# A new hand-order table for an RWKV-5 block fused with a squared-ReLU MLP: same steps, other engine orders, PSUM banks, fillers and squares

## The chip, the cores and the metric

One core of a Trainium2 chip runs the whole program. The metric is the device time of one execution in microseconds: of the kernel before, the median of three runs. Five engines work side by side, each through its own list of instructions in order: TensorE (PE; its weight loads are PEld), VectorE (DVE), ScalarE (ACT), GpSimd (POOL) and SyncE (SP). SP does nothing here but start transfers; POOL and ACT start some too. All transfers of the core share 16 DMA engines. Matrix products land in PSUM, eight banks of 128 partitions by 512 floats; the other operands lie in SBUF.

## The reference

First an attention-like recurrence over 768 steps for 4 batches and 8 heads of 48 columns, then a two-layer MLP on its 3072 rows:

```python
for t in range(S):
    cur = np.einsum('bhd,bhe->bhde', u[None] * kt, vt)
    y[:, :, t] = np.einsum('bhd,bhde->bhe', rt, state + cur)
    state = w[None, :, :, None] * state + np.einsum('bhd,bhe->bhde', kt, vt)
...
h = x @ w_in            # 3072 x 384 by 384 x 2048
g = np.maximum(h, 0.0) ** 2
return g @ w_out        # 2048 x 384
```

Inputs and output are float32.

## The kernel before

**Tiling.** The 768 steps are cut into 6 chunks of 128; a chunk of one batch is a *unit*, and there are 24 of them, numbered chunk by chunk (units 0 to 3 are the four batches of chunk 0). Within a unit the recurrence is done in matrix form: r and k are scaled by powers of w (`scale`, L301/L303), turned so that the head's columns lie on partitions (`turn` and `rkT` through PE and ACT for units 0 to 5; one transposing transfer `rkD`, L322, for a pair of units from 6 on), multiplied into a 128 by 128 table per head (`at`, L369), masked to its triangle (`mask`, L377), multiplied with v (`y`, L441) and with the state of the chunks before (L447). `rk` and `d` (L357/L360, L389/L410) give the diagonal that u weights, `dv` (L420) and `yb` (L456) add it, and `s`, `sadd`, `sdec`, `stb` (L398, L424, L428, L432) carry the state on. `xturn`/`xT` or the transposing transfer `xD` (L467) turn y into the MLP's input. `m1` (L493) is the first product, `relu` (L501, ACT) takes it out of PSUM as f32, the square goes to ACT (`sqA`, L508) or DVE (`sqD`, L510), `m2` (L517) is the second product in four quarters per unit, `osb` (L524, ACT) takes its 128 by 384 result out, and `out` (L553, SP) stores it. Unit 23, the last, has its second product in two pieces (`m2.23.0`, `m2.23.1`, L533) with an eviction each (`osb.23.0` on ACT, L543; `osb.23.1` on DVE, L545) and a store each (`out.23.0`, `out.23.1`, L549).

**What sets the order.** Nothing is scheduled by the compiler: the string `ORDER` lists every step as a word, and the loop at the end of the kernel runs through it and issues the step's instructions. Each engine executes its own instructions in the order in which their words stand; words of different engines only wait for each other through the data. `name.unit.part@banks` gives the PSUM bank of a matmul step. `fill.N` issues N matmuls on a constant tile whose result nobody reads (L216). An instruction that isn't ready holds all that stands behind it on its engine. That goes for SP too: a store waits there for its eviction, and every later transfer of SP waits behind it.

**Buffers.** Evicted output rows (`osb`) rotate through 6 SBUF buffers, evicted hidden tiles (`gr`) through 6, loaded pairs of r, k and v through 4. An eviction `osb` that gets a buffer for the second time waits until the store of the former content has landed. The `osb` of the two pieces of unit 23 have one buffer each of their own.

```python
mpool = ctx.enter_context(tc.tile_pool(name="mpool", bufs=6))
...
tiles[i]["osb"] = mpool.tile([128, dm], F32, name="osb")
nc.scalar.copy(tiles[i]["osb"], tiles[i]["o"])
...
nc.sync.dma_start(out=out[b * S + c * C : b * S + (c + 1) * C, :], in_=tiles[i]["osb"])
```

Of the kernel before, what the change touches and what calls it, by code (L numbers as in the profile page):

```python
# [26 lines left out]
relu.0.1 s.3@7 xT.2 d.3@6 sqD.0.1 at.3@40 relu.1.1 turn.4.1@2 mask.3.1 m1.2.2@1 vb.4 rkT.4.1 dv.3 m1.2.3@5 relu.2.2
mask.3.0 at.4@02 vb.5 rk.4 m2.0.0@6 relu.2.3 mask.4.0 sqA.2.2 m1.2.1@1 sqD.2.3 relu.1.3 m1.2.0@4 mask.4.1 sqA.0.2
sqD.1.3 m2.1.0@5 stb.2 relu.2.0 sadd.3 kb.4@0 y.3@3 relu.2.1 sqD.1.1 y.4@2 stb.3 m2.0.1 yb.3 kbT.4 scale.5.0 m2.1.1
sqA.2.0 sqD.2.1 kt.8 xturn.3@4 s.4@7 xT.3 turn.5.0@1 sadd.4 m2.1.2 rkT.5.0 dv.4 m1.3.1@3 sdec.4 kt.10 yb.4 m1.3.0@0  # L30
stb.4 relu.3.1 scale.6.0 m2.0.2 scale.5.1 relu.3.0 xturn.4@4 scale.7.0 m2.0.3 sqA.3.0 rt.8 sqD.3.1 xT.4 m1.3.3@1
osb.0 scale.6.1 turn.5.1@7 out.0 relu.3.3 m1.4.0@2 scale.7.1 rkT.5.1 m2.3.0@3 sqD.3.3 relu.4.0 rkD.6 m1.4.3@0 rk.5
sqA.4.0 kb.5@4 relu.4.3 at.5@61 m1.4.2@7 kbT.5 mask.5.0 vtS.6 m1.4.1@2 sqD.4.3 relu.4.2 mask.5.1 m2.3.1 sqA.4.2
s.5@0 relu.4.1 y.5@4 dv.5 m2.1.3 sqA.4.1 vtS.8 sadd.5 m1.3.2@6 yb.5 osb.1 sdec.5 out.1 relu.3.2 m2.2.0@7 scale.8.0
stb.5 scale.8.1 m2.2.1 rt.10 sqA.3.2 scale.9.0 m2.2.2 scale.9.1 m2.2.3 m2.3.2 osb.2 rkD.8 rk.6 at.6@1205 xturn.5@4
mask.7.1 m2.4.0@6 xT.5 out.2 mask.6.1 m2.4.1 vb.6 mask.7.0 rt.12 m1.5.3@7 mask.6.0 s.6@5 relu.5.3 s.7@4 dv.6 y.7@2
y.6@0 dv.7 m2.4.2 sqD.5.3 vtS.10 vb.8 m1.5.0@1 yb.6 yb.7 m2.4.3 relu.5.0 sadd.7 xD.6 m1.5.1@7 scale.10.0 sqA.5.0
scale.10.1 m2.3.3 osb.4 relu.5.1 sdec.7 out.4 m1.5.2@0 scale.11.1 osb.3 stb.7 m2.5.0@2 scale.11.0 sqA.5.1 sadd.6
out.3 at.8@1467 relu.5.2 rk.8 rkD.10 m2.5.1 sqA.5.2 mask.8.0 s.8@3 mask.8.1 s.9@5 kt.12 m2.5.2 sdec.6 y.8@0 sadd.8
stb.6 m2.5.3 scale.12.0 mask.9.0 osb.5 sadd.9 out.5 mask.9.1 kt.14 vb.10 m1.6.0@1 sdec.9 dv.8 m1.6.4@4 relu.6.0  # L40
scale.13.0 m1.6.3@2 yb.8 vtS.12 sqA.6.0 sdec.8 m1.6.6@6 relu.6.4 dv.9 relu.6.3 m1.6.7@7 sqA.6.4 sqD.6.3 m1.6.1@3
relu.6.7 rk.10 rt.14 y.9@1 relu.6.6 m1.6.2@0 sqD.6.7 stb.9 relu.6.1 yb.9 at.10@4527 relu.6.2 scale.12.1 s.11@6 xD.8
m1.6.5@3 sqA.6.1 mask.11.1 sqA.6.2 s.10@1 dv.11 m2.6.0@0 vtS.14 relu.6.5 dv.10 m2.6.1 scale.13.1 sqA.6.6 mask.10.0
sqA.6.5 m2.7.0@7 stb.8 rkD.12 mask.11.0 m2.7.1 mask.10.1 m2.7.2 sadd.10 vb.12 m2.6.2 sadd.11 kt.16 sdec.10 m2.6.3
sdec.11 y.10@3 osb.6 y.11@4 stb.10 yb.10 out.6 m2.7.3 stb.11 yb.11 m1.8.0@2 scale.14.0 osb.7 xD.10 scale.14.1
m1.8.1@5 relu.8.0 scale.15.0 m1.8.7@1 scale.15.1 sqA.8.0 out.7 m1.8.3@6 relu.8.1 kt.18 relu.8.7 m1.8.2@0 sqA.8.1
kt.20 sqD.8.7 m1.8.6@3 relu.8.2 m2.8.0@4 relu.8.3 sqA.8.2 m1.8.4@7 sqD.8.3 relu.8.6 at.12@2510 rk.12 relu.8.4 m2.8.1
mask.13.1 sqA.8.6 rkD.14 s.12@6 mask.12.0 sqA.8.4 m1.8.5@3 vb.14 mask.12.1 s.13@7 m1.10.5@0 relu.8.5 sadd.12 rt.16
sadd.13 y.12@2 sqA.8.5 sdec.12 m1.10.6@5 relu.10.5 sdec.13 m2.8.2 stb.12 mask.13.0 sqA.10.5 m1.10.3@3 vtS.16 dv.13
relu.10.6 m1.10.0@0 dv.12 relu.10.3 yb.12 m1.10.1@1 sqA.10.6 sqD.10.3 relu.10.0 y.13@7 vtS.18 m1.10.7@5 relu.10.1  # L50
yb.13 sqA.10.0 m2.8.3 xD.12 relu.10.7 m1.10.4@6 osb.8 sqD.10.7 stb.13 m1.10.2@3 out.8 rk.14 relu.10.4 at.14@2017
vtS.20 relu.10.2 m2.9.0@5 sqA.10.4 mask.14.0 sqA.10.2 s.15@4 mask.15.1 m2.9.1 sqA.10.1 dv.15 rt.18 m2.9.2 sadd.15
m2.11.0@6 mask.15.0 vb.16 sdec.15 m2.11.1 scale.16.0 m2.11.2 scale.16.1 rt.20 m2.11.3 scale.17.0 mask.14.1 s.14@3
osb.11 y.15@2 dv.14 m2.9.3 vb.18 out.11 sadd.14 rt.22 stb.15 y.14@7 scale.17.1 osb.9 m1.12.0@4 sdec.14 out.9
m1.12.7@1 yb.14 stb.14 yb.15 relu.12.0 m1.12.3@0 relu.12.7 rkD.16 m1.12.2@6 sqA.12.0 sqD.12.7 m1.12.1@3 relu.12.3
xD.14 relu.12.2 m1.12.4@5 sqD.12.3 relu.12.1 scale.18.0 m1.12.6@7 sqA.12.2 scale.18.1 m1.12.5@2 sqA.12.1 scale.19.0
m2.10.0@4 relu.12.4 vtS.22 scale.19.1 relu.12.5 scale.20.0 m2.13.0@1 sqA.12.4 scale.20.1 m2.10.1 scale.21.0 sqA.12.5
m2.13.1 scale.21.1 vb.20 rkD.18 m2.10.2 relu.12.6 m2.10.3 sqA.12.6 scale.22.0 m2.13.2 osb.10 scale.23.0 rkD.20
m2.13.3 m2.12.0@0 osb.13 m2.12.1 rk.16 out.13 out.10 at.16@6352 kt.22 s.16@7 mask.17.0 m1.14.5@4 sadd.16 m1.14.1@1
relu.14.5 dv.16 s.17@5 vb.22 mask.16.0 m2.12.2 dv.17 relu.14.1 m1.14.2@4 sadd.17 sqA.14.5 m1.14.7@7 mask.16.1  # L60
sqA.14.1 sdec.17 m1.14.0@6 relu.14.2 sdec.16 relu.14.7 y.16@1 rk.18 sqA.14.2 m1.14.4@5 yb.16 relu.14.0 m2.12.3
sqD.14.7 relu.14.4 m1.14.6@3 osb.12 mask.17.1 sqA.14.4 m1.14.3@4 out.12 rk.20 sqA.14.0 y.17@7 relu.14.3 at.18@1650
yb.17 stb.17 m2.15.0@2 sqD.14.3 xD.16 relu.14.6 mask.18.0 s.21@4 stb.16 m2.14.0@7 sqA.14.6 dv.21 m2.15.1 mask.18.1
s.18@3 mask.19.0 m2.15.2 sadd.18 m2.15.3 dv.18 y.18@1 osb.15 sdec.18 m2.14.1 yb.18 out.15 stb.18 m2.14.2 scale.22.1
mask.19.1 m2.14.3 scale.23.1 s.20@4 s.19@6 osb.14 dv.20 at.20@5321 rkD.22 dv.19 y.19@0 mask.20.0 m1.16.0@7 mask.21.1
out.14 m1.16.2@4 relu.16.0 yb.19 m1.16.1@5 sqA.16.0 mask.21.0 xD.18 m1.16.5@1 relu.16.2 mask.20.1 relu.16.1
m1.16.3@7 sadd.19 relu.16.5 y.21@0 sdec.19 sqA.16.1 m1.16.7@2 stb.19 y.20@4 relu.16.3 m2.16.0@3 yb.20 sqA.16.2
m1.16.6@5 sqD.16.3 relu.16.7 sqA.16.5 yb.21 m1.16.4@6 sqD.16.7 relu.16.6 xD.20 m2.17.0@1 relu.16.4 rk.22 m2.17.1
sqA.16.6 at.22@7420 sqA.16.4 s.22@5 m1.18.4@6 mask.23.0 mask.23.1 m2.17.2 relu.18.4 dv.22 m1.18.6@2 sqA.18.4
mask.22.0 y.23@0 relu.18.6 mask.22.1 m1.18.7@6 sqA.18.6 s.23@5 m1.18.1@7 dv.23 relu.18.7 m1.18.3@2 sqD.18.7  # L70
relu.18.1 m1.18.2@4 sqA.18.1 m1.18.5@5 relu.18.3 relu.18.2 y.22@6 sqD.18.3 m1.18.0@7 relu.18.5 yb.22 sqA.18.2
# [551 lines left out]
```

## Time and profile before

| | |
|---|---|
| three runs, median (lowest to highest) | 174.9 us (174.62 to 177.03) |
| the profiled execution, its own time | 173.95 us |
| its span, first to last instruction | 172.2 us |
| PE busy | 165.0 us (96%) |
| DVE / ACT / POOL busy | 121.9 / 131.4 / 15.9 us |
| HBM read / written | 20.50 / 4.72 MB |

The views used are: the page (a summary with the span cut into 40 slices), groups of instructions by line, tables of busy time by stretch, the timeline, the chain of waits that ended last, and SP's own rows, where a row's duration is the time that the sequencer spent on starting a transfer. A matmul row's duration counts from its issue to the end of its drain, so that neighbouring matmuls overlap and a busy PE may still be waiting a little.

### The profile page before, as it was taken

What the parts mean: (1) busy time and instruction counts of PE and PEld (TensorE: products, weight loads), DVE (VectorE), ACT (ScalarE), POOL (GpSimd) and SP (SyncE); (2) the same over time, 40 slices, a digit from 0 to 9 for tenths busy, and PEclk for the clock granted to TensorE, in tenths of its full rate; (3) what the DMA queues carried; (4) which work ended last, traced back from release to release, by engine and by line L of the source; (5) the groups of instructions that cost most, each with busy time, mean ns of one, the idle gap of its engine ahead of it and who ended that gap; (6) DMA issues with size and microseconds to landing.
All of it is one profiled execution on the core that took longest, in us unless ns stands there. A gap on an engine that the chain in (4) does not pass through costs nothing.

```text
span 172.2 us, 4759 instructions
## 1 busy us (share of the span) xinstructions
PE 165.0 (96%) x1964; PEld 135.8 (79%) x1964; DVE 121.9 (71%) x243; ACT 131.4 (76%) x255; POOL 15.9 (9%) x36
## 2 busy tenths in 40 slices
PE   7989899999999999999979999999999999999992
...
PEclk9999999999999999999999999999999999999999
...
GB/s 95 180 289 235 277 235 216 209 197 243 154 247 222 247 194 236 203 173 251 168 227 230 186 201 245 165 239 212 46 213 50 0 25 116 0 46 49 0 127 58
DMA packets 91493, 28.86 MB, mean 168 GB/s; under 512 B 82864, under 2 KB 90672, under 8 KB 91472
## 3 DMA queue, kind: packets, MB, share of 16 engines
...
q0 software_dynamic: 2624, 4.33, 12.4%
q10 hardware_dynamic: 432, 0.25, 0.6%
...
HBM read 20.50 MB, written 4.72 MB: 146 GB/s over the span
## 4 chain that ended last, share of the span: by engine, by line
PE 81%; DMA 8%; DVE 4%; ACT 2%; SPq 2%; issue 1%; DVEq 0%
PE bank L517 34%; PE bank L493 31%; DMA rkT<-rkw 5%; DMA rt<-in_r_dram 4%; PE bank L369 3%; PE bank L441 2%; PE bank L398 2%; PE bank L447 2%; SPq L281 2%; PE bank L533 2%; PE bank L410 1%; PE bank L333 1%; PE bank L216 1%; DVE rkw L303 1%; DVE am L377 1%
## 5 line engine op out<-in xcount | busy, mean ns | idle before, releaser
L493 PE MATMUL bank<-xT,w_in_q 128*128 128x256 bf16 (+1 forms) x720 | 72.1, 251 | 0.0
L517 PE MATMUL bank<-w_out_q,g 128*128 128x384 bf16 x368 | 67.6, 326 | 0.0
L493 PEld LDWEIGHTS <-w_in_q 128*128 128x128 bf16 x720 | 64.0, 113 | 3.3
L501 ACT ACTIVATE gr<-bank 128x512 f32<-128x512 f32 x96 | 55.1, 603 | 10.0 <-PE bank L493 9.8
L517 PEld LDWEIGHTS <-g 128*128 128x128 bf16 x368 | 34.3, 98 | 18.3
L508 ACT ACTIVATE g<-gr 128x512 bf16<-128x512 f32 x68 | 42.0, 640 | 0.8
L510 DVE TENSOR_TENSOR g<-gr 128x512 bf16<-128x512 f32 x28 | 19.3, 688 | 24.1 <-ACT gr L501 23.9
L377 DVE TENSOR_TENSOR am<-bank,smask 128x512 bf16<-128x512 f32 x48 | 31.5, 683 | 3.8 <-PE bank L369 3.7
L524 ACT COPY osb<-bank 128x384 f32<-128x384 f32 x23 | 11.0, 479 | 10.7 <-PE bank L517 10.6
L456 DVE TENSOR_TENSOR yb<-bank,dv 128x384 bf16<-128x384 f32 x24 | 12.9, 551 | 1.0 <-PE bank L447 0.8
L420 DVE TENSOR_TENSOR dv<-vb,bank 128x384 f32<-128x384 bf16 x24 | 12.8, 547 | 0.9 <-PE bank L398 0.5
L432 ACT CAST stb<-st 128x384 bf16<-128x384 f32 x20 | 10.4, 523 | 3.1 <-DVE st L428 3.0
L216 PE MATMUL bank<-warm 128*128 128x128 bf16 x104 | 10.3, 269 | 1.1 <-DVE warm L161 1.1
L301 DVE TENSOR_TENSOR rkw<-rt,wpos 128x384 bf16<-128x384 f32 x18 | 9.8, 551 | 0.8 <-DMA rt<-in_r_dram 0.8
L316 ACT CAST vb<-vt 128x768 bf16<-128x768 f32 x9 | 7.6, 841 | 3.4 <-DMA vt<-in_v_dram 3.4
L301 DVE TENSOR_TENSOR rkw<-kt,wneg 128x384 bf16<-128x384 f32 x18 | 9.8, 550 | 0.0
L216 PEld LDWEIGHTS <-warm 128*128 128x128 bf16 x104 | 8.7, 124 | 1.2 <-DVE warm L161 1.0
L369 PE MATMUL bank<-rkT 64*128 64x128 bf16 x192 | 8.0, 219 | 0.9 <-DMA rkT<-rkw 0.9
L424 DVE TENSOR_TENSOR st<-bank,st 128x384 f32<-128x384 f32 x16 | 8.6, 550 | 0.2 <-PE bank L398 0.2
L441 PE MATMUL bank<-vb,am 128*128 128x48 bf16 x192 | 8.7, 183 | 0.0
L357 DVE TENSOR_TENSOR rk<-rkT 128x1024 bf16<-128x1024 bf16 x9 | 6.2, 686 | 3.4 <-DMA rkT<-rkw 3.4
L428 DVE TENSOR_TENSOR st<-st,wend 128x384 f32<-128x384 f32 x16 | 8.6, 551 | 0.0
...
## 6 DMA issues: line engine op xcount, KB each, us to landing
out_dram<-osb SPq DMA_DIRECT2D x23, 192.0 KB, 2.3
...
w_out_q<-in_moe_w_out_dram POOLq DMA_DIRECT2D x4, 384.0 KB, 13.0
vt<-in_v_dram POOLq DMA_DIRECT2D x6, 192.0 KB, 7.3
...
```

The source lines that it names most:

```text
L216: nc.tensor.matmul(out=banks[0][:, :128], lhsT=warm, rhs=warm, start=True, stop=True)
L301: nc.vector.tensor_tensor(t["rkw"][:, x, :, :, :D], pair(src), pair(wneg if x else wpos), ALU.mult)
L369: nc.tensor.matmul(out=t["at"][o][:, p, :], lhsT=t["rkT"][sl, 1, p, :], rhs=t["rkT"][sl, 0, p, :], start=True, stop=True,)
L377: nc.vector.tensor_tensor(am, t["at"][o], smask.unsqueeze(1).to_broadcast([C, HP, C]), ALU.mult)
L420: nc.vector.tensor_tensor(t["dv"], t["vb"], t["d"].unsqueeze(2).to_broadcast([C, H, D]), ALU.mult)
L441: nc.tensor.matmul(out=y[:, 2 * p + o, :], lhsT=t[f"am{o}"][:, p, :], rhs=t["vb"][:, 2 * p + o, :], start=(o == 0 and p == 0), stop=c == 0 ...
L456: nc.vector.tensor_tensor(t["yb"], t["y"], t["dv"].rearrange("p h d -> p (h d)"), ALU.add)
L493: nc.tensor.matmul(out=t["h", s][:, a], lhsT=turned, rhs=chunks[c]["xT"][:, b : b + m, n, :], start=(n == 0), stop=(n == NK - 1),)
L501: nc.scalar.activation(t["gr", s], t["h", s], AF.Relu)
L508: nc.scalar.activation(g, x, AF.Square)
L510: nc.vector.tensor_tensor(g, x, x, ALU.mult)
L517: nc.tensor.matmul(out=t["o"], lhsT=chunks[units[i][0]]["g"][:, f, units[i][1], :], rhs=w_out_q[f // 4][:, f % 4, :], start=(f == 0), stop ...
```

## The change

`ORDER` alone differs; no function does. The steps are the same ones: 96 first products, 68 squares on ACT and 28 on DVE, 94 quarters or pieces of the second product, 25 evictions and stores, the same loads and turns. What differs is the order of the words, and with it of each engine's instructions, the bank numbers, which squares go to which engine, and the fillers: 104 matmuls in ten places before, 64 in eight after. The beginning and the end of the table:

```diff
-kt.0.0 kt.0.1 rt.0.0 rt.1.0 I.0 rt.1.1 ids fill.25 log@4567 ktA.1.0 lnat.0 rt.2.0 vt.0 lnat.1 w.0 fill.1 cols@1
-kt.1.1 w.1 upper copied kt.2.0 end scale.0.0 wk kt.2.1 vt.1 scale.0.1 wr fill.14 turn.0.0@2 rt.2.1 turn.0.1@3 zeros
-rkT.0.0 rt.3.0 vt.2 rkT.0.1 scale.1.0 rt.3.1 uwb fill.16 at.0@14 rk.0 kb.0@5 mask.0.1 turn.1.0@6 I.3 kbT.0 rt.4.0
-mask.0.0 fill.4 d.0@7 rkT.1.0 I.2 vb.0 vb.1 rt.4.1 dv.0 wend fill.17 s.0@2 y.0@3 scale.1.1 kt.3.0 vb.2 vt.3 yb.0
-kt.3.1 fill.13 turn.1.1@4 sadd.0 I.1 rkT.1.1 kt.4.0 fill.4 xturn.0@5 xT.0 rk.1 vt.4 kt.4.1 fill.8 kb.1@1 stb.0
-scale.2.0 at.1@67 kbT.1 kt.5.0 d.1@3 scale.2.1 m1.0.0@2 vt.5 mask.1.0 rt.5.0 s.1@4 turn.2.0@5 relu.0.0 mask.1.1 O.0
-turn.2.1@1 rkT.2.0 fill.2 m1.0.3@6 sadd.1 O.3 rt.5.1 sqA.0.0 dv.1 y.1@0 relu.0.3 scale.3.0 O.1 rt.6 yb.1 stb.1
...
-sqA.18.2 m2.16.1 yb.23 sqA.18.5 m2.16.2 xD.22 relu.18.0 m2.16.3 sqA.18.0 m2.17.3 osb.16 m1.20.0@2 out.16 osb.17 m2.19.0@4
-out.17 relu.20.0 m2.19.1 sqA.20.0 m1.20.4@5 m1.20.7@6 relu.20.4 m2.18.0@0 sqA.20.4 m1.20.1@7 relu.20.7 m1.20.6@3
...
-sqD.22.3 m2.20.3 m1.22.6@0 osb.20 m2.21.3 out.20 relu.22.6 m2.22.0@1 sqA.22.6 m2.22.1 osb.21 out.21 m2.22.2 m2.22.3
-m2.23.0@4 osb.22 out.22 m2.23.1@5 osb.23.0 out.23.0 osb.23.1 out.23.1
+kt.0.0 kt.0.1 rt.0.0 rt.1.0 I.0 rt.1.1 ids ktA.1.0 lnat.0 fill.17 log@4567 kt.1.1 upper lnat.1 cols@1 rt.2.0 w.1
+zeros w.0 rt.2.1 wk vt.0 scale.0.0 kt.2.0 scale.0.1 wr fill.10 turn.0.0@3 kt.2.1 copied uwb turn.0.1@1 rkT.0.0
+rt.3.0 rkT.0.1 vt.1 rk.0 fill.6 at.0@15 scale.1.0 rt.3.1 I.3 d.0@6 mask.0.0 fill.2 turn.1.0@4 I.2 kb.0@3 kt.3.0
+mask.0.1 rkT.1.0 vt.2 scale.1.1 vb.0 I.1 kt.3.1 fill.14 turn.1.1@1 dv.0 y.0@7 rkT.1.1 rt.4.0 yb.0 vt.3 kbT.0 rk.1
+fill.8 kb.1@4 rt.4.1 scale.2.0 at.1@72 vt.4 kbT.1 xturn.0@6 kt.4.0 mask.1.0 d.1@3 turn.2.0@1 xT.0 rkT.2.0 scale.2.1
+kt.4.1 fill.4 m1.0.0@6 end mask.1.1 vb.1 turn.2.1@1 wend kt.5.0 rkT.2.1 dv.1 fill.3 y.1@4 m1.0.3@2 relu.0.0 vt.5
+yb.1 rt.5.0 kb.2@5 rk.2 relu.0.3 at.2@73 scale.3.0 O.0 s.0@1 sqA.0.0 mask.2.1 xturn.1@6 kt.5.1 turn.3.0@2 O.1 xT.1
...
+m1.20.0@4 sqD.18.7 dv.23 m1.20.3@2 m1.20.1@6 relu.20.3 y.23@7 sqA.18.5 sqD.20.3 m1.20.6@5 relu.20.1 yb.23 m1.20.5@2
+sqA.18.0 xD.22 osb.17 m1.20.2@7 relu.20.0 m1.20.7@3 sqA.18.2 m2.16.3 relu.20.6 relu.20.5 m2.19.0@6 osb.16 m2.19.1
...
+sqA.22.1 m2.21.3 sqA.22.4 m1.22.5@0 osb.21 m2.20.1 relu.22.5 m2.20.2 sqA.22.0 m1.22.2@3 m2.22.0@1 relu.22.2 m2.18.3
+sqA.22.2 m2.20.3 sqA.22.5 m2.22.1 m2.22.2 m2.23.0@2 m2.22.3 m2.23.1@0 osb.23.1 out.23.1 out.14 out.15 out.17 osb.18
+osb.20 osb.22 osb.23.0 out.23.0 out.22 out.16 out.21 out.20 out.18 out.19
```

SP's words from the first transposing transfer on, taken out of the two tables (`vtS` is a load of v, `rkD` and `xD` are transposing transfers):

```
before: rkD.6 vtS.6 vtS.8 out.1 rt.10 rkD.8 out.2 rt.12 vtS.10 xD.6 out.4 out.3 rkD.10 kt.12 out.5 kt.14 vtS.12 rt.14
        xD.8 vtS.14 rkD.12 kt.16 out.6 xD.10 out.7 kt.18 kt.20 rkD.14 rt.16 vtS.16 vtS.18 xD.12 out.8 vtS.20 rt.18 rt.20
        out.11 rt.22 out.9 rkD.16 xD.14 vtS.22 rkD.18 rkD.20 out.13 out.10 kt.22 out.12 xD.16 out.15 rkD.22 out.14
        xD.18 xD.20 xD.22 out.16 out.17 out.19 out.18 out.20 out.21 out.22 out.23.0 out.23.1
after:  rkD.6 kt.10 vtS.8 rt.10 rkD.8 out.2 vtS.10 xD.6 rt.12 kt.12 rkD.10 rt.14 vtS.12 xD.8 out.1 out.0 kt.14 kt.16
        rkD.12 rt.16 xD.10 out.4 vtS.14 rkD.14 kt.18 rt.18 vtS.16 xD.12 rt.20 out.3 kt.20 rkD.16 out.5 xD.14 vtS.18
        rt.22 out.6 out.11 out.7 kt.22 rkD.18 out.9 rkD.20 xD.16 vtS.20 out.8 out.12 vtS.22 rkD.22 xD.18 out.13 xD.20
        out.10 xD.22 out.23.1 out.14 out.15 out.17 out.23.0 out.22 out.16 out.21 out.20 out.18 out.19
```

(`out.0` stands ahead of `rkD.6` in the table before.) The `osb` evictions stand on ACT in the order 0 1 2 4 3 5 7 6 8 9 11 10 13 12 14 15 17 16 19 21 18 20 22 23.0 after.

More of the change, by code (lines that the diff above doesn't have):

```diff
@@ L27 @@
[L27 to L71, printed above, removed]
@@ new lines @@
+xturn.3@6 sqD.1.3 m2.0.1 xT.3 relu.2.3 s.4@7 m2.1.1 stb.1 sqD.2.3 relu.2.1 m1.3.0@0 sadd.4 relu.2.2 m2.1.2 scale.5.1
+relu.3.0 scale.5.0 rt.8 m2.0.2 sqA.2.2 dv.4 sqA.2.0 turn.5.0@5 y.4@0 rkT.5.0 turn.5.1@7 yb.4 m2.0.3 sqD.2.1 kt.8
+m2.1.3 osb.0 scale.6.0 rkT.5.1 xturn.4@0 m1.3.3@6 scale.7.0 osb.1 xT.4 m1.3.2@7 vtS.6 relu.3.3 at.5@02 vb.5
+scale.6.1 kb.5@1 m2.2.0@6 scale.7.1 kbT.5 sdec.4 sqA.3.0 m1.3.1@4 rkD.6 mask.5.0 stb.2 m1.4.0@1 relu.3.1 m1.4.2@3
+stb.4 scale.8.0 relu.4.0 m2.3.0@4 mask.5.1 relu.4.2 sqD.3.1 m2.2.1 kt.10 sqA.4.2 rk.5 m2.2.2 relu.3.2 sqD.3.3
@@ new lines @@
+sqA.4.0 s.5@0 m1.4.3@5 vtS.8 sadd.5 dv.5 y.5@1 relu.4.3 m2.3.1 scale.9.0 sqA.3.2 scale.8.1 m1.4.1@7 yb.5 rt.10
+m2.2.3 scale.9.1 relu.4.1 m2.4.0@5 sqD.4.3 stb.3 sqA.4.1 sdec.5 xturn.5@7 at.6@2310 vb.6 rk.6 rkD.8 m2.4.1 osb.2
+mask.7.1 xT.5 m2.3.2 mask.6.0 s.7@7 mask.6.1 s.6@0 m2.4.2 dv.6 y.6@2 mask.7.0 out.2 m1.5.3@3 vb.8 sadd.6 vtS.10
+y.7@6 dv.7 relu.5.3 m1.5.0@1 yb.6 yb.7 m2.4.3 relu.5.0 scale.10.0 xD.6 m1.5.1@2 osb.4 scale.10.1 stb.5 m2.3.3
+scale.11.1 relu.5.1 rt.12 scale.11.0 m1.5.2@6 sqA.5.0 rk.8 sqA.5.1 at.8@0312 kt.12 osb.3 m2.5.0@5 mask.8.1 relu.5.2
@@ new lines @@
+s.8@4 sqD.5.3 sqA.5.2 m2.5.1 sdec.6 vb.10 s.9@3 rkD.10 mask.9.1 m2.5.2 dv.8 m2.5.3 mask.8.0 m1.6.3@6 osb.5 dv.9
+stb.6 m1.6.0@2 sadd.8 relu.6.3 rt.14 mask.9.0 m1.6.1@5 relu.6.0 sadd.9 y.8@0 sqA.6.0 y.9@4 yb.8 vtS.12 relu.6.1
+m1.6.7@2 yb.9 m1.6.2@3 sdec.9 relu.6.7 xD.8 sadd.7 m1.6.6@5 sqA.6.1 scale.12.0 relu.6.2 m1.6.5@2 sqD.6.3 out.1
+sqA.6.2 m2.6.0@0 out.0 rk.10 relu.6.6 kt.14 m1.6.4@7 scale.13.0 sqA.6.6 sqD.6.7 at.10@5461 relu.6.5 m2.7.0@3
+mask.11.0 sqA.6.5 kt.16 m2.6.1 mask.11.1 relu.6.4 s.11@2 scale.12.1 sqA.6.4 m2.7.1 scale.13.1 s.10@1 sdec.7 m2.7.2
@@ new lines @@
+sadd.10 stb.7 m2.6.2 rkD.12 sadd.11 m2.7.3 sdec.8 mask.10.1 m1.8.0@7 mask.10.0 m1.8.3@6 relu.8.0 sdec.10 m2.6.3
+vb.12 rt.16 dv.10 y.10@4 relu.8.3 dv.11 y.11@7 osb.7 yb.10 m1.8.1@5 sqA.8.0 scale.14.0 m1.8.2@2 yb.11 relu.8.1
+scale.15.0 m1.8.6@1 osb.6 xD.10 sqD.8.3 relu.8.2 m1.8.5@7 relu.8.6 scale.14.1 m1.8.4@0 relu.8.5 scale.15.1 out.4
+m1.8.7@4 sqA.8.1 vtS.14 rk.12 relu.8.4 at.12@6251 rkD.14 sqA.8.2 m2.9.0@7 mask.12.0 stb.9 s.12@0 sqA.8.6 mask.13.1
+m2.8.0@3 stb.8 mask.13.0 m2.8.1 sqA.8.5 mask.12.1 sqA.8.4 m1.10.6@6 kt.18 dv.12 relu.8.7 m1.10.1@1 scale.16.0
@@ new lines @@
+relu.10.6 sadd.12 rt.18 m1.10.3@5 relu.10.1 scale.16.1 m2.8.2 sqA.10.1 sdec.11 s.13@6 scale.17.1 relu.10.3 y.13@1
+sqD.8.7 sqA.10.6 y.12@2 vtS.16 m1.10.5@5 dv.13 yb.12 m2.8.3 relu.10.5 sadd.13 m1.10.7@0 vb.14 sdec.13 m1.10.2@6
+yb.13 relu.10.7 sdec.12 m1.10.0@2 xD.12 osb.8 rk.14 m2.9.1 relu.10.0 scale.17.0 at.14@5031 rt.20 relu.10.2 sqA.10.0
+m2.9.2 out.3 mask.14.1 stb.11 kt.20 s.15@6 mask.15.1 sqA.10.2 s.14@4 m2.11.0@2 sqD.10.3 stb.10 m2.10.0@1 mask.14.0
+rkD.16 m2.9.3 mask.15.0 sadd.15 m2.11.1 osb.9 dv.15 stb.12 y.15@5 scale.18.0 m2.10.1 dv.14 m1.10.4@3 scale.18.1
```

34 lines of the change are left out of this document (26 added, 8 removed).

## The prediction

> **What bounds the kernel now.** I read the summary page first, for which engine is busy and when.
>
> ```profile
> span 172.2 us, 4759 instructions
> ...
> PE   7989899999999999999979999999999999999992
> ...
> PEclk9999999999999999999999999999999999999999
> ```
>
> PE is at nine tenths or more in nearly every slice after the first few; only the last is almost empty. The table of busy time by stretch makes this exact (columns: us, then busy time and instruction count of PE, PEld, DVE, ACT, POOL, then clock, DMA share, GB/s):
>
> ```profile
> 0.00:20.00 20.00, 17.41 (x243) 15.60 (x244) 14.19 (x41) 13.12 (x28) 15.93 (x36) 1.00 0.96 208
> 20.00:80.00 60.00, 59.84 (x826) 49.24 (x825) 54.54 (x105) 50.17 (x100) 0.00 (x0) 1.00 1.14 219
> 80.00:90.00 10.00, 9.05 (x112) 7.99 (x111) 7.57 (x15) 9.96 (x20) 0.00 (x0) 1.00 1.13 196
> 90.00:140.00 50.00, 50.00 (x568) 40.70 (x566) 42.07 (x80) 36.66 (x71) 0.00 (x0) 1.00 0.76 156
> 140.00:168.75 28.75, 28.73 (x225) 22.26 (x222) 3.24 (x6) 21.47 (x40) 0.00 (x0) 1.00 0.16 56
> 168.75:172.20 3.45, 0.00 (x0) 0.00 (x0) 0.29 (x1) 0.00 (x0) 0.00 (x0) 1.00 0.18 59
> ```
>
> So there are three parts. A start of 20 us, where PE runs fillers and waits; 148.75 us in which PE idles 1.1 us in all; and 3.45 us after the last matmul. What PE still waited for after 20 us, by the view of waits:
>
> ```profile
> PE bank L369 <- DMA rkT<-rkw: 0.9, 1, 0.9
> PE bank L410 <- DVE rk L357: 0.2, 1, 0.2
> ```
>
> The time is therefore the moment when PE ends plus the tail behind it. The end of the chain that ended last:
>
> ```profile
> 162.85 3.25 PE bank L517 x20
> 166.10 2.65 PE bank L533 x32
> 168.77 0.29 DVE osb L545
> ```
>
> PE ends at 166.10 + 2.65 = 168.75. A table with the same steps and 40 fillers fewer can change the end only through the start, through new or lost stalls in the middle, and through the tail. I take the tail first: it moves most.
>
> **The tail.** SP's own rows in the timeline, its waits, and the starts and landings of its last stores:
>
> ```profile
> 142.51 24.46 SPq L553 DMA_DIRECT2D out_dram<-osb  x7
> 168.28 1.15 SPq L549 DMA_DIRECT2D out_dram<-osb  x2
> ```
>
> ```profile
> SPq L553 <- ACT osb L524: 25.2, 8, 7.9
> ```
>
> ```profile
> L553 SPq DMA_DIRECT2D out_dram<-osb x7: 332/332/338, 142.5 to 166.6; - x7
> L549 SPq DMA_DIRECT2D out_dram<-osb x2: 332/332/332, 168.3 to 169.1; - x2
> ...
> DMA to landing us min/median/max: 1.8/1.8/2.8
> ```
>
> Before, SP starts each of the last stores when its eviction is ready: seven from 142.5 to 166.6, then the two pieces. It waits in order: 25.2 us in 8 waits for evictions, with nothing of SP started meanwhile. In the new table `out.23.1` stands directly behind `xD.22`, and behind it ten stores: 14, 15, 17, 23.0, 22, 16, 21, 20, 18, 19. `out.23.1` waits for `osb.23.1`, which waits for the last matmul. So ten stores that could have gone under PE's work start after it has ended.
>
> A second wait hangs on it. There are six `osb` buffers; in ACT's new order `osb.18` is the 21st eviction and takes the buffer of the 15th, `osb.14`; likewise `osb.20` that of 15 and `osb.22` that of 17. So these three evictions wait until `out.14`, `out.15` and `out.17` have landed, and `osb.23.0` stands behind them on ACT. Nothing else is behind them: no matmul reuses their banks, so PE isn't held up.
>
> The prices, from issue groups, eviction groups and a stretch in which only stores move:
>
> ```profile
> 114.40 1.00 SPq L553 DMA_DIRECT2D out_dram<-osb  x2
> ```
>
> ```profile
> out_dram<-osb SPq DMA_DIRECT2D x23, 192.0 KB, 2.3
> ```
>
> ```profile
> 167.88 0.37 ACT L543 COPY osb<-bank 128x256 f32<-128x256 f32 x1 [1.27 <-PE bank L533]
> ```
>
> ```profile
> L524 ACT COPY osb<-bank 128x384 f32<-128x384 f32 x23 | 11.0, 479 | 10.7 <-PE bank L517 10.6
> ```
>
> ```profile
> 142.50:146.30 3.80, 3.80 (x31) 3.08 (x30) 0.00 (x0) 2.71 (x5) 0.00 (x0) 1.00 0.28 104
> ```
>
> Two stores that were ready started 0.5 us apart (1.00 for two). A store lands 1.8 us (last ones) to 2.3 us (median) after its start; I take 2.05. 104 GB/s at a share of 0.28 makes 371 GB/s at full share, 0.53 us for 196,608 bytes, so rate and starts limit about equally. From the end of PE:
>
> - DVE evicts `osb.23.1`: 0.02 + 0.29 = 0.31. `out.23.1` starts at 0.34, `out.14` at 0.84, `out.15` at 1.34, `out.17` at 1.84.
> - They land at 2.9, 3.4 and 3.9. `osb.18` ends at 2.9 + 0.48 = 3.4, `osb.20` at 3.9, `osb.22` at 4.4, `osb.23.0` at 4.4 + 0.37 = 4.75.
> - `out.23.0` starts at 4.8 and six more follow at 0.5 us: the last starts at 7.8 and lands at 9.85.
> - Before, the last store started at 169.1; a landing of 2.1 (the faster of the two pieces in the row below) makes 171.2, and the span ended at 172.2. That is 1.0 us from landing to end, which stays: 10.85 us.
>
> ```profile
> DMA to landing us min/median/max: 2.1/2.4/2.8
> ```
>
> Against 3.45 that is **+7.4 us**. With the shortest starts (0.35) and landings (1.8) the last landing is at 8.25: +5.8. With 0.55 and 2.8 it is 11.8: +9.3.
>
> **The start.** Three rows of the chain, and two of PE's timeline:
>
> ```profile
> 3.64 6.47 DMA rt<-in_r_dram
> 10.21 0.57 DVE rkw L303
> ...
> 17.50 0.46 DVE dv L420
> 18.13 0.22 issue
> 18.34 0.56 DVE yb L456
> ```
>
> The chain leaves the load of r for unit 1 at 10.11 and is then mostly DVE's list up to `yb.1`. In the new list `rk.0` stands ahead of `scale.1.0`, in time that DVE spent waiting for that load, and `sadd.0`, `sadd.1` and `scale.3.0` stand behind `yb.1`. That is four instructions fewer on the chain at about 0.46 each (the `dv` row): 1.8 us at most. Against it: the load of v for unit 0 is moved behind the triangle and two memsets on POOL, so `vb.0` and `dv.0` may come late, and the loads of the first units arrive in SP's order at a DMA share of 0.96. I take −1.0 and keep −1.8 to +1.5. The 40 fillers are worth nothing themselves: they stand in waits, which stay.
>
> ```profile
> 7.53 1.91 PE L216 MATMUL bank<-warm 128*128 128x128 bf16 x16
> ...
> 11.39 1.11 PE L216 MATMUL bank<-warm 128*128 128x128 bf16 x17
> ```
>
> They have a second use. Sixteen fillers took 1.91 us at 7.5 us (119 ns each), seventeen took 1.11 at 11.4 (65 ns): between them PE doubled its rate, though the page's clock row says full speed throughout. The new table has 16 fillers in front of `at.0` after the first ones, where 31 stood. If the rate doubles later, the work from `turn.1.0` to the first `m1` runs at half speed.
>
> The Trainium skill, "TensorE: Matmul & The Clock Gate", Part 1 (the clock gate), says that the clock is halved until the array has been busy for a window of some 3.4 us, and that the window runs freely. The trace agrees in the two rates. By that rule the thinner filling could open the gate later; what that would cost is in the second case below.
>
> **The middle.** Two things move. The one lasting stall was for a transposed pair:
>
> ```profile
> 81.08 7.86 DMA rkT<-rkw
> ```
>
> `rkD.14` took 7.86 us to land and PE waited 0.9 for it. By that point SP's new list has 4 stores behind it instead of 8; four stores at 0.53 are 2.1 us of a DMA share that stood above 1.1. The stall should go: −0.9. Nothing comes late in its place that I can name: `at.8` and `at.12` have less PE work between their `rkD` and themselves than before, but also fewer stores ahead.
>
> The banks are tighter. For each matmul step that takes a bank, I added the PE work that stands in the table between the word that empties the bank and the step, with the lengths of the chain's rows:
>
> ```profile
> 149.14 0.65 PE bank L493 x6
> 149.79 0.65 PE bank L517 x4
> ```
>
> From `at.4` on, 2 steps before have under 0.7 us, and 33 after; under 1.2 us, 15 and 55. An eviction needs about that long:
>
> ```profile
> L501 ACT ACTIVATE gr<-bank 128x512 f32<-128x512 f32 x96 | 55.1, 603 | 10.0 <-PE bank L493 9.8
> ...
> L493 PE MATMUL bank<-xT,w_in_q 128*128 128x256 bf16 x432 | 52.7, 273 | 0.0
> ```
>
> A relu takes 0.60 and can begin only when the last matmul has drained, 0.273 − 0.65/6 = 0.16 after its turn. At a distance of 0.65 PE would be 0.11 short: 31 new places, 3.4 us. But a PE that has waited once finds the next bank empty, and ACT and DVE have idle time to catch up. I take +1.9, between 0 and 4. The squares' split (68 and 28) is the same, so ACT's and DVE's sums stay.
>
> **Sum.** Start −1.0, stall −0.9, banks +1.9: PE ends where it did. Tail +7.4. On the profiled execution's own 173.95 us (span 172.2) this gives 181.35. That execution lay 0.95 under the median of the three runs, 174.9; carried to the median it is 182.3. I say **181.5**, nearer to the traced run, since 174.62 was reached too.
>
> **The rivals.**
>
> - *Forecast, 0.68*: tail +5.8 to +9.3 with PE's end moved by no more than about 2: 178.5 to 185.
> - *PE falls back, 0.15*: the tight banks cost their full 3.4 us, or the half rate lasts. From `turn.1.0` to the first `m1` and its turns the new table has about 4.2 us of PE work at full rate (26 of its fillers 1.45, the rest by the 0.65 row scaled to its columns); at half rate it is 4.2 more, partly under DVE's chain, so 2 to 4. With the tail 184.5 to 188. For it: 33 against 2. Against: before, the places with 0.65 show no wait in the view.
> - *Not slower, 0.13*: the front chain pays for the tail. Four DVE instructions (1.8) and the stall (0.9) go, the banks cost nothing, so PE ends 2.7 early, and the tail takes its lower 5.8: +3.1, 177.0 on the traced run and 178.0 on the median. It decides from the point where tail less PE's advance falls under 3.5 us (2% of 174.9, which is about what a measurement of this kernel can tell from no change). Against it: that needs both ends at once. Faster by over 2% would need PE 10.9 us earlier at a tail of 7.4, and after 20 us PE has only 1.1 us to give.
> - *The stores don't queue, 0.04*: that what stands behind `out.23.1` starts anyway, so the tail stays 3.45 and the time is 173 to 176. SP's 25.2 us of waits in order speak against it.
>
> **How the numbers follow.** Slower by over 2%: the first two, 0.83. Within: most of the last two, 0.14. Faster: 0.03. The range leaves out half of each outer case: 177.5 to 187.
>
> **What would show it.** In the changed kernel's trace: ten store rows on SP after the last matmul, at distances near 0.5 us; three ACT evictions ended by a landing and not by PE; 10 to 11 us from PE's last matmul to the end of the span, where 3.45 stood. PE's last matmul within 2 us of 168.75. A rkT wait that is gone, and small new waits of `m1` and `m2` rows for ACT or DVE. Wrong would be a tail under 7, a PE end beyond 171, or waits over a microsecond in the middle: then the banks or the clock were mis-sized.

## The result and the profile after

The changed kernel takes **180.0 us** (median of 6 runs, 179.34 to 180.72) beside 175.1 of the kernel before on the same chip; the ratio is 1.030, 95% interval 1.024 to 1.036. The forecast was 181.5, slower by over 2%, and the time lies in its range (177.5 to 187). The profiled execution took 179.34 us, with a span of 177.6. The ratios here and below leave out executions that took over 1.5% longer than the fastest of their kernel; the medians and ranges count all of them.

The page of the changed kernel: the span in 40 slices, and two groups of ACT (busy us, mean ns | idle us before, and what ended it).

```profile
PE   5889999999999999999999999999999999999600
...
PEclk9999999999999999999999999999999999999975
DMA  3999999999999999989989999999504050000047
...
L501 ACT ACTIVATE gr<-bank 128x512 f32<-128x512 f32 x96 | 55.6, 602 | 18.9 <-PE bank L493 14.5
...
L524 ACT COPY osb<-bank 128x384 f32<-128x384 f32 x23 | 11.1, 482 | 10.9 <-DMA out_dram<-osb 7.5
```

PE is empty in the last two slices and part of the one before them, and just there the DMA row rises again. (The lower clock at the end stands over an idle PE.) The table by stretch has the same columns as before; the last stretch begins where PE's last matmul ends, at 167.2:

```profile
0.00:20.00 20.00, 17.18 (x216) 14.77 (x216) 14.04 (x40) 11.80 (x25) 15.65 (x36) 1.00 0.96 209
20.00:80.00 60.00, 60.00 (x822) 49.27 (x819) 55.36 (x106) 50.09 (x101) 0.12 (x1) 1.00 1.07 207
80.00:90.00 10.00, 9.86 (x126) 8.27 (x125) 9.14 (x19) 8.63 (x18) 0.00 (x0) 1.00 0.99 191
90.00:140.00 50.00, 49.88 (x548) 40.39 (x547) 39.38 (x74) 38.74 (x77) 0.00 (x0) 1.00 0.82 163
140.00:167.20 27.20, 27.19 (x225) 21.41 (x223) 4.20 (x7) 18.27 (x36) 0.00 (x0) 1.00 0.10 9
167.20:177.60 10.40, 0.00 (x0) 0.00 (x0) 0.29 (x1) 1.71 (x4) 0.00 (x0) 0.69 0.51 189
```

From 20 us to 167.2 PE idles 0.27 us in all; the view of waits lists no wait of PE after 18 us. PE ends 1.55 us earlier than before (168.75), and the tail is 10.40 us where 3.45 stood: +6.95. The sum, +5.4, is the difference of the two spans (177.6 − 172.2) and of the two profiled times (179.34 − 173.95).

The tail in the timeline of the changed kernel (start, us, engine, line, operation; in brackets the idle time before and what ended it):

```profile
167.30 0.29 DVE L545 COPY osb<-bank 128x128 f32<-128x128 f32 x1 [10.79 <-PE bank L533]
167.62 0.34 SPq L549 DMA_DIRECT2D out_dram<-osb  x1
168.05 1.36 SPq L553 DMA_DIRECT2D out_dram<-osb  x3
170.00 1.47 ACT L524 COPY osb<-bank 128x384 f32<-128x384 f32 x3 [7.54 <-DMA out_dram<-osb]
171.37 0.38 ACT L543 COPY osb<-bank 128x256 f32<-128x256 f32 x1
171.77 0.33 SPq L549 DMA_DIRECT2D out_dram<-osb  x1
172.16 2.92 SPq L553 DMA_DIRECT2D out_dram<-osb  x6
```

```profile
L553 SPq DMA_DIRECT2D out_dram<-osb x9: 382/441/460, 168.0 to 174.6; - x9
...
DMA to landing us min/median/max: 1.9/2.0/2.0
```

```profile
SPq L549 <- DVE osb L545: 23.1, 1, 23.1
```

The last row is SP's own wait: it stands 23.1 us in front of `out.23.1`, with nothing started. Then come eleven stores after the last matmul, that one and the ten queued behind it; ACT stands 7.54 us until the second of them, `out.14`, has landed at 169.9, evicts three results and the first piece of unit 23, and SP starts the last store at 174.6. It lands 2.0 later, and the span ends 1.0 after that.

### The profile page after: what moved, and what is told of

It reads as the page before. It is cut to its first block, busy times and chain, and to the rows that moved or that the text cites. A ratio compares the mean times of both kernels' runs of the same rounds, so it can differ in the third digit from the quotient of the medians.

```text
span 177.6 us, 4694 instructions
## 1 busy us (share of the span) xinstructions
PE 164.1 (92%) x1924; PEld 134.1 (76%) x1924; DVE 122.4 (69%) x243; ACT 129.2 (73%) x255; POOL 15.8 (9%) x36
## 4 chain that ended last, share of the span: by engine, by line
PE 81%; DMA 12%; SPq 2%; ACT 1%; DVE 0%; issue 0%; ACTq 0%; DVEq 0%
PE bank L493 32%; PE bank L517 31%; DMA rkT<-rkw 4%; PE bank L369 3%; DMA rt<-in_r_dram 3%; DMA xT<-yb 3%; PE bank L441 3%; PE bank L398 2%; PE bank L447 2%; PE bank L333 2%; PE bank L216 2%; PE bank L533 1%; SPq L281 1%; PE bank L345 1%; DMA out_dram<-osb 1%; PE bank L410 1%
## 5 line engine op out<-in xcount | busy, mean ns | idle before, releaser
L501 ACT ACTIVATE gr<-bank 128x512 f32<-128x512 f32 x96 | 55.6, 602 | 18.9 <-PE bank L493 14.5
L517 PE MATMUL bank<-w_out_q,g 128*128 128x384 bf16 x368 | 69.3, 326 | 0.0
L510 DVE TENSOR_TENSOR g<-gr 128x512 bf16<-128x512 f32 x28 | 19.1, 687 | 14.1 <-ACT gr L501 14.1
L337 ACT COPY rkT<-bank 128x512 bf16<-128x512 bf16 x12 | 7.0, 593 | 4.0 <-PE bank L333 4.0
L216 PE MATMUL bank<-warm 128*128 128x128 bf16 x64 | 7.9, 301 | 1.1 <-DVE warm L161 1.1
L441 PEld LDWEIGHTS <-am 128*128 128x128 bf16 x192 | 7.9, 97 | 0.8
```

Source lines behind the costliest of these rows:

```text
L216: nc.tensor.matmul(out=banks[0][:, :128], lhsT=warm, rhs=warm, start=True, stop=True)
L441: nc.tensor.matmul(out=y[:, 2 * p + o, :], lhsT=t[f"am{o}"][:, p, :], rhs=t["vb"][:, 2 * p + o, :], start=(o == 0 and p == 0), stop=c == 0 ...
L501: nc.scalar.activation(t["gr", s], t["h", s], AF.Relu)
L510: nc.vector.tensor_tensor(g, x, x, ALU.mult)
L517: nc.tensor.matmul(out=t["o"], lhsT=chunks[units[i][0]]["g"][:, f, units[i][1], :], rhs=w_out_q[f // 4][:, f % 4, :], start=(f == 0), stop ...
```

## The experiments

"New table" is the changed kernel. All were compared with the kernel before on the same chip; span, end of PE and tail (span less end of PE) are those of the one profiled execution.

| kernel | median us | ratio, 95% interval | span | PE ends | tail |
|---|---|---|---|---|---|
| new table | 180.0 | 1.030 (1.024 to 1.036) | 177.6 | 167.2 | 10.4 |
| a0 new table once more | 180.5 | 1.031 (1.024 to 1.037) | 179.0 | 168.65 | 10.35 |
| a1 its stores back | 173.8 | 0.995 (0.990 to 1.000) | 171.3 | 168.4 | 2.9 |
| a2 three free buffers | 178.6 | 1.023 (1.015 to 1.031) | 176.9 | 168.7 | 8.2 |
| b1 late stores in the table before | 181.2 | 1.038 (1.029 to 1.046) | 179.1 | 168.6 | 10.5 |
| b2 four stores later, table before | 175.3 | 1.006 (1.001 to 1.010) | 173.4 | 170.5 | 2.9 |
| a3 a1, ten fillers more | 173.4 | 0.989 (0.984 to 0.995) | 171.7 | 168.8 | 2.9 |
| a4 a1, no fillers | 171.9 | 0.980 (0.975 to 0.986) | 169.6 | 166.65 | 2.95 |
| a5 a1, two groups of fillers out | 172.3 | 0.988 (0.982 to 0.994) | 170.4 | 167.5 | 2.9 |
| c1 a1, two loads later | 172.9 | 0.985 (0.980 to 0.990) | 171.2 | 168.3 | 2.9 |
| d1 a4 and c1 | 171.9 | 0.985 (0.980 to 0.989) | 170.7 | 167.8 | 2.9 |
| b3 table before, no fillers | 175.3 | 1.003 (1.000 to 1.007) | 172.9 | 169.5 | 3.4 |

The theory was that the late stores are the whole loss; the rival, that part of it is something else in the new order (banks, the rate of PE) which an early front hides.

### a1: the stores back behind their evictions

```diff
 osb.14 +out.14    osb.15 +out.15    osb.17 +out.17    osb.16 +out.16    osb.19 +out.19    osb.21 +out.21
-m2.23.1@0 osb.23.1 out.23.1 out.14 out.15 out.17 osb.18
-osb.20 osb.22 osb.23.0 out.23.0 out.22 out.16 out.21 out.20 out.18 out.19
+m2.23.1@0 osb.18 out.18 osb.20 out.20 osb.23.0 out.23.0 osb.22 out.22 osb.23.1 out.23.1
```

> The new table with its ten late stores put back behind their evictions, and osb.18, osb.20 and osb.22 ahead of osb.23.1; nothing else moves. Tail theory: the new table's PE ends at 167.2 us as it does now, and the tail falls back to the 3.4 us of the kernel before: span 170.7, time about 172.5, 1.5% under the kernel before. Rival, that part of the 5.2 us sits in the banks or in the half rate of the start: PE ends later than 168.75 or the time stays at 175 or above.

The words `osb.18`, `osb.20` and `osb.22` keep their order on ACT (`osb.23.0` now stands ahead of `osb.22`), but nothing holds them. Of the stores, `out.23.1` alone starts after PE's end:

```profile
168.53 0.29 DVE L545 COPY osb<-bank 128x128 f32<-128x128 f32 x1 [10.78 <-PE bank L533]
168.85 0.33 SPq L549 DMA_DIRECT2D out_dram<-osb  x1
```

The tail falls from 10.4 to 2.9 and the time to 173.8, the time of the kernel before or a little under it. So the late stores are the whole loss, and the rest of the new order gains between nothing and 1%. The expected 172.5 wasn't reached: PE ended at 168.4 and not at 167.2, since `at.12` waited 1.9 us for `rkD.12`, which took 7.51 us to land. Run a0 takes this up.

### b1: the late stores in the table before

```diff
-...out.15 ...out.14 ...out.16 ...out.17 ...out.19 ...out.18 ...osb.20 out.20 ...osb.21 out.21
-m2.23.0@4 osb.22 out.22 m2.23.1@5 osb.23.0 out.23.0 osb.23.1 out.23.1
+m2.23.0@4 m2.23.1@5 osb.23.1 out.23.1 out.15 out.14 out.16 osb.20 osb.21 osb.22 osb.23.0
+out.23.0 out.22 out.17 out.21 out.20 out.18 out.19
```

> The table of before with the new tail alone: stores 14 to 19 and the evictions and stores 20 to 23.0 put behind out.23.1 in the new table's manner (osb.20, osb.21 and osb.22 then wait for the landings of out.15, out.14 and out.16). Tail theory: PE ends at 168.75 as before, the tail is 10.4 us: span 179.1, time about 181, 6.9 us slower than before. Rival, that the stores matter through the DMA share in the middle: PE's end moves by over 1 us as well.

The counterpart: the change's end alone, on the kernel before. Its timeline after the last matmul:

```profile
168.98 0.34 SPq L549 DMA_DIRECT2D out_dram<-osb  x1
169.41 1.36 SPq L553 DMA_DIRECT2D out_dram<-osb  x3
171.32 1.52 ACT L524 COPY osb<-bank 128x384 f32<-128x384 f32 x3 [7.29 <-DMA out_dram<-osb]
172.74 0.38 ACT L543 COPY osb<-bank 128x256 f32<-128x256 f32 x1
173.14 0.33 SPq L549 DMA_DIRECT2D out_dram<-osb  x1
173.53 2.93 SPq L553 DMA_DIRECT2D out_dram<-osb  x6
```

These rows are those of the changed kernel, 1.4 us later. PE's end hasn't moved (168.6 against 168.75), and the span is 6.9 longer than before. Beside the end of the table before, the new end costs about 7.0 us of tail in either table (10.5 and 10.4 against 3.45). Beside a1's end, whose tail is 2.9, it costs 7.5.

### a2: the buffer wait taken away

```diff
-tiles[i]["osb"] = mpool.tile([128, dm], F32, name="osb")
+tiles[i]["osb"] = mpool.tile([128, 512], F32, name="gr")[:, :dm] if i in (18, 20, 22) else mpool.tile(...)
```

> The new table as it is, but osb.18, osb.20 and osb.22 take free gr buffers, so that they no longer wait for a landing; the ten stores still stand behind out.23.1. Tail theory, which has two parts: the ten starts alone, at 0.48 us apart, put the last start 4.7 us behind PE's end and the span's end 7.7 behind it: span 174.9, time 176.7, 2.7 us less than the new table (3.3 us faster). If the buffer wait is the lesser part, under 1 us is gained; if the transfer rate limits and not the chain of evictions, nothing is gained.

The new table, with `osb.18`, `osb.20` and `osb.22` in `gr` buffers that are free by then. The stores stay late.

```profile
167.87 0.48 ACT L524 COPY gr<-bank 128x384 f32<-128x384 f32 x1 [3.12 <-PE bank L517]
168.25 0.38 ACT L543 COPY osb<-bank 128x256 f32<-128x256 f32 x1
168.83 0.29 DVE L545 COPY osb<-bank 128x128 f32<-128x128 f32 x1 [10.79 <-PE bank L533]
169.15 0.34 SPq L549 DMA_DIRECT2D out_dram<-osb  x1
169.58 1.36 SPq L553 DMA_DIRECT2D out_dram<-osb  x3
171.03 0.41 SPq L549 DMA_DIRECT2D out_dram<-osb  x1
...
173.99 0.46 SPq L553 DMA_DIRECT2D out_dram<-osb  x1
```

ACT's evictions now end before PE does, and the eleven stores start one after the other. The tail is 8.2: of the 6.95 us, the queue on SP is 4.7 (8.2 − 3.45) and the buffers are 2.2 (10.4 − 8.2). This rests on the tails, which differ by 0.15 us at most between the two executions of the new table and b1; in time over the runs (178.6 against 180.0) the intervals of the two ratios overlap. The span is 2 us longer than was expected all the same: 0.5 of it is tail (7.7 was expected), and 1.5 came because PE ended later in this execution, after a wait of 1.3 us ahead of `at.10`. The view of waits names ACT for that wait, but `rkD.10` took 7.6 us and landed at 67.17, and `at.10` began at 67.22. The next run has such a wait without the free buffers.

### a0: the new table once more

> The new table unchanged, once more. In the runs so far PE's end lay at 167.2, 168.4 and 168.7 us with the same words up to 115 us, and a wait of 1.3 to 1.9 us for one transposing transfer made the difference. Theory that this is chance of the transfers' timing: PE ends anywhere from 167 to 169.5, the tail is 10.4 again within 0.2, the time 179.3 to 181. Rival, that the first run's early end is the new table's own: PE ends at 167.2 within 0.3.

The same tail, but PE ends at 168.65 and not at 167.2. The rows below are PE's only waits after 18 us (two, 1.7 and 0.4), and the transposing transfers (min, median, max), first of this run and then of the changed kernel's first execution:

```profile
PE bank L369 <- DMA rkT<-rkw: 2.1, 2, 1.7
```

```profile
DMA to landing us min/median/max: 5.1/6.1/8.0
```

```profile
DMA to landing us min/median/max: 4.9/5.5/7.9
```

`rkD.12` landed in 7.54 us here and in 5.74 in the first execution. The same program in two executions, so 1.5 us of PE's end is chance; differences of that size between single profiles prove nothing below.

### b2: four stores behind rkD.14 in the table before

```diff
 osb.3 -out.3    osb.5 -out.5    osb.6 -out.6    osb.7 -out.7
-rkD.14
+rkD.14 out.3 out.5 out.6 out.7
```

> The table of before with out.3, out.5, out.6 and out.7 put behind rkD.14, so that four stores fewer stand ahead of that transposing transfer. Theory that the stall at rkD.14 goes because stores moved: rkD.14 lands 1 to 2 us earlier, PE's 0.9 us wait for it goes, PE ends at about 168.0 and the time falls by 0.7 us. Rival, that the stall comes from when rkD.14 can start (its scaled input) or from the loads ahead of it: the wait stays.

This is the prediction's reason for the stall that goes, alone. `rkD.14` landed at 87.2 instead of 88.9 (it started 0.7 us earlier and took 6.8 us instead of 7.9), and PE's 0.9 us for it went. But the time did not follow; PE waits elsewhere instead:

```profile
PE bank L441 <- ACT gr L501: 0.9, 1, 0.9
...
PE bank L517 <- ACT g L508: 0.6, 1, 0.6
```

`vtS.22` landed at 112.5 instead of 110.6, ACT stood 2.4 us for it, and PE behind ACT. The stall went as argued, in this one execution, and was given back at a later transfer. That the moved stores made `vtS.22` late is not shown: it took 5.3 us here, 3.8 in the kernel before and in b1, and 5.2 in b3, where no store has moved.

### a3, a4, b3, a5: what the fillers are worth

Three edits of a1 and one of the kernel before:

```diff
 a3:  -fill.6 +fill.9    -fill.2 +fill.9
 a4:  -fill.17 -fill.10 -fill.6 -fill.2 -fill.14 -fill.8 -fill.4 -fill.3
 a5:  -fill.14 -fill.8
 b3:  -fill.25 -fill.1 -fill.14 -fill.16 -fill.4 -fill.17 -fill.13 -fill.4 -fill.8 -fill.2
```

> The new table with its stores put back, and 10 fillers more (9 instead of 6 ahead of at.0, 9 instead of 2 ahead of turn.1.0), so that PE has no gap between 5.5 us and the first m1. Theory that unbroken work opens the gate: the distance of fillers falls from 107 to 56 ns by 10 us, as in the kernel before, where it fell at 14.3 us in the new table. Whether it is worth anything: if PE's steps were on the chain, at.2 comes 0.5 to 1 us earlier; if DVE's list sets it, at.2 stays at 18.0 within the 0.4 that runs differ by.

> The new table with its stores put back and no filler at all. Theory that fillers only open the gate: the rate stays halved until the first m1 steps have filled a window, to about 18 to 20 us; at.2 comes 0.5 to 2 us later and PE's end with it, time 1 to 2 us above the version with stores put back. Rival, that they are worth nothing since the waits stay: at.2 within 0.4 of 18.0.

In a1, as in the new table, PE runs at half rate until about 14 us; PE's timeline of a1:

```profile
10.58 1.70 PE L216 MATMUL bank<-warm 128*128 128x128 bf16 x14
12.08 0.63 PE L333 MATMUL bank<-identb,rkw 128*128 128x128 bf16 x4
12.50 0.53 PE L441 MATMUL bank<-vb,am 128*128 128x48 bf16 x8
12.86 1.03 PE L216 MATMUL bank<-warm 128*128 128x128 bf16 x8
```

With ten fillers more (a3) the rate doubles at about 10.5 us; `at.1` begins at 13.8 and `at.2` at 17.4, 0.3 us earlier each than in a1 (14.1 and 17.8), although `turn.1.0`, behind its load, began 0.95 later (10.71 against 9.76). Without any (a4) it doubles only at 16.0, and the kernel is the fastest of all but for d1's equal time: 171.9 us. The expectation, a loss of 1 to 2 us, was wrong. PE's timeline of a4:

```profile
11.10 0.61 PE L333 MATMUL bank<-identb,rkw 128*128 128x128 bf16 x4 [0.63 <-DVE rkw L303]
11.78 0.48 PE L441 MATMUL bank<-vb,am 128*128 128x48 bf16 x8
12.38 0.61 PE L345 MATMUL bank<-identb,rkT 128*128 128x128 bf16 x4
13.03 0.61 PE L369 MATMUL bank<-rkT 64*128 64x128 bf16 x8
```

`turn.1.1` (L333) begins 1.0 us earlier than in a1, where PE was still busy with the fourteen fillers, and it waits for its data there: the fillers overran the wait that they were to fill. Of the 1.8 us by which PE ends earlier, 0.4 stand at `at.2`; the rest is a wait of 1.9 for `rkD.12` in a1 that a4's execution didn't have (it had one of 0.5 for `xD`). The intervals of a4 and a1 do not meet, so the gain is there. That the fillers make it is not shown, and c1 and d1 below speak against it: with the fillers and without them, both with the same two loads moved, the ratio is 0.985.

> Edit: the new table with the stores back behind their evictions, and without two of its groups of fillers, the 14 and the 8 ahead of the first turns of unit 1. Theory (these two groups, 1.5 and 0.86 us at half rate, are the ones that stand on the chain): turn.1.1 and at.1 about 1 us earlier than with all fillers (at.1 at 13.3 to 13.5 against 14.3), the time about 172 to 172.8. Rival (the gain without fillers comes from other groups, or from loads that happened to land earlier): at.1 stays at 14.3 and the time at 173.4 to 174.

`at.1` begins at 13.2, 0.9 us earlier than in a1, as this theory had it: the two groups do stand on the chain. The lead was lost at once, though. PE's timeline of a5:

```profile
10.17 0.39 PE L345 MATMUL bank<-identb,rkT 128*128 128x128 bf16 x4
11.60 0.40 PE L333 MATMUL bank<-identb,rkw 128*128 128x128 bf16 x4 [1.04 <-DVE rkw L303]
...
12.67 0.61 PE L345 MATMUL bank<-identb,rkT 128*128 128x128 bf16 x4 [0.42 <-ACT rkT L337]
...
15.00 1.49 PE L493 MATMUL bank<-xT,w_in_q 128*128 128x128 bf16 x12
```

In this execution the rate doubled at about 8.6 us, fell back to half at 12.0 and doubled again at 18.8. The clock shows this drop, in the row of a5's page and in the table by stretch (last but two of the columns):

```profile
PEclk9995799999999999999999999999999999999999
```

```profile
8.55:11.96 3.41, 1.51 (x30) 1.06 (x26) 2.73 (x6) 1.07 (x2) 3.41 (x5) 1.00 1.12 313
11.97:18.78 6.81, 6.39 (x77) 5.87 (x74) 4.96 (x11) 4.31 (x10) 4.43 (x8) 0.50 1.17 235
```

In the 3.41 us ahead of the drop PE was busy for 1.51; it stood idle 1.04 us in front of `turn.1.1`, where a1 has the fourteen fillers. `at.2` came 1.3 us later than in a1. PE ended earlier in the end since no transposed pair was late. So a5's 172.3 us does not say what the two groups cost.

> Edit: the kernel before with no filling matmuls at all. Theory (fillers cost where they run at half rate on the chain, and in the kernel before the rate doubles at about 9.5 us, so that most of them run at full rate and in waits): the rate doubles at about 16 us, at.2 stands 0 to 1 us from where it was, and the time moves by -1 to +1 us (174 to 176). Rival (fillers pay by the early doubling of the rate): the first units run at half rate, at.2 0.5 to 2 us later, the time 176 to 177. Second rival (fillers cost wherever they stand): 172 to 173.5, as in the new table.

In the kernel before, all 104 fillers are worth 0.3% (interval 0.0 to 0.7%), as the first theory had it. But `at.2` comes 1.4 us later without them, more than it allowed, and the half rate lasts to about 18. A part of this was hidden: PE came later to `at.14` and found `rkD.14` landed, where the kernel before waits 0.9 us, and it ended 0.75 later.

### c1 and d1: two loads behind the transposing transfers

```diff
-at.8@0312 kt.12 ... rkD.10
+at.8@0312 ... rkD.10 kt.12
-sqA.6.5 kt.16 ... rkD.12
+sqA.6.5 ... rkD.12 kt.16
```

> The new table with its stores put back, and the loads kt.12 and kt.16 put behind rkD.10 and rkD.12, whose results PE waited for in two of three runs. Theory that these transfers are late because of what stands ahead of them in the DMA queues: both land 1.5 to 2 us earlier, at.10 and at.12 wait no more, PE ends at 167 and the span at 170.2: time 172, 1.7% under the kernel before. Rival, that their time varies by itself: waits as before, time 173.8.

> Edit: the new table with the stores back behind their evictions, without its fillers, and with the loads kt.12 and kt.16 issued behind the transposing loads rkD.10 and rkD.12. Theory (the half-rate fillers stand on the chain of the first units; the two loads crowd the transposing transfers): both gains show together, PE's last matmul ends at about 166.5, the span is about 169.5, the time 171.8, ratio 0.98 or a little below. Rival (the transposing transfers take 5 or 7.5 us by chance, and moving the loads does nothing): 171.8 as without fillers alone in some runs, up to 173 in others, and the profiled run may show a wait of 1 to 2 us for rkT.

In c1 `rkD.10` and `rkD.12` landed in 5.3 and 5.6 us and PE waits for neither. But this execution's start was late (first row: c1's only wait of PE over half a microsecond after the first 5 us), and so was d1's (second row):

```profile
PE bank L333 <- DVE rkw L303: 1.8, 1, 1.8
```

```profile
PE bank L333 <- DVE rkw L303: 2.2, 2, 1.6
```

That is the load of r for unit 1. In d1 its second half landed at 9.9 us, in a4, whose loads up to there are the same, at 8.7; and PE's rate doubled at 19.1 in d1, where it did at 16.0 in a4. The two gains don't add up: d1 is as fast as a4 and not faster, its ratio is that of c1, which has all the fillers, and PE's end at 166.5, which was expected, wasn't reached. In medians over runs both stay under a1; a1 to c1 the intervals just touch. The best versions, a4 and d1, beat both kernels: 1.5 to 2% under the kernel before, and some 8 us under the changed one.

## Why the prediction was right

- **The tail**, forecast +7.4, measured +6.95, and alone in the old table 6.9 (b1). The mechanism was right in each step: ten stores behind `out.23.1`, three evictions that wait for landings, `osb.23.0` behind them. The first four stores started 0.43 to 0.48 apart and not 0.5, and the three that the evictions wait for landed in 1.88 to 1.92 us and not in 2.05; the last six started 0.49 apart. So the last one started 7.4 us after PE's end and not 7.8. The end of the span came 1.0 after the last landing, as before.
- **The stall**, −0.9: `rkD.14` landed in 5.5 us instead of 7.9, and PE did not wait. The reason (fewer stores) has b2 for it: 6.8 us, against 7.9, 7.2 and 7.7 in the three executions with the old order of stores there (before, b1, b3). This is one execution, though, and in d1, with the new order, `rkD.14` took 7.3. b2 also shows that such a gain can be given back, and a0 that another transfer may be late by chance instead.
- **The start**, −1.0. Let a step's lag be the time at which PE reaches it less the useful PE work ahead of it in the table (all but the fillers, at the full rate). It fell from 13.2 to 12.4 at `at.2`, from 13.4 to 12.9 at `at.4`, from 15.65 to 14.0 at `at.14` and from 16.9 to 15.4 at the end. So the start gave 0.5 to 0.8 us and what follows, the stall in it, the rest: together −1.55 where −1.9 was forecast. That the four DVE instructions made the start's part is not shown. b1 has the words of the table before up to unit 18, and it reached `at.4` at 26.99 us where the kernel before did at 27.54, as much earlier as the new table's lag; its r for unit 1 landed at 8.9 us, against 10.1 before and 9.2 in the new table.
- **The banks**, +1.9, is the term that was mis-sized: some tenths at most. No wait of PE over 0.2 us is left after 18 us, although 33 places have under 0.7 us from the word that empties the bank to the step. From `at.4` to the end the lag grew by 2.5 us, and before by 3.5, of which the two waits that the view lists there are 1.1: what is left is the same (2.5 and 2.4). The page of the changed kernel shows ACT waiting for PE in front of `relu` for 14.5 us, against 9.8 before, so ACT often stood ready when PE had drained; that this is the reason is argued, not shown. The estimate charged each place 0.11 us, the difference of two rounded sums, and this is within what such a sum can tell. No run varied the banks alone.
- **The fillers**, "worth nothing themselves: they stand in waits, which stay": right in size for the old table (b3, 0.3%), wrong as a reason for the new one. At half rate fourteen fillers take 1.5 us and run past the wait; `at.1` came 0.9 to 1.1 us earlier without them (a5, a4). What this is worth at the end stays open (a4 against a1, but d1 against c1).
- **The half rate**, priced at 2 to 4 us in the rival: the rate did double later, at 14.2 us instead of 9.5, and `at.1` was still 0.5 earlier than before. PE's end did not fall back; that rival is out, and so is that of stores that don't queue. The rival "not slower" had the banks right, but PE came 1.55 early and not 2.7, and the tail was 6.95 and not 5.8.

On the traced run the forecast was 181.35 and 179.34 came: banks −1.9, tail −0.45, start and stall +0.35. That PE's end came near the forecast's 168.75 has luck in it: in a0 it lay at 168.65, by a wait of 1.7 us for `rkD.12` and not by waits for banks. The tail, which alone makes the loss, came by its own mechanism.
